# A zero tile for the warm-up products, bn_stats for block 3's second norm, and a new order of operations in an attention and MLP kernel

## The chip, the cores and the metric

The kernel runs on one core of one Trainium2 chip. The metric is device time in microseconds (us), the median over several executions of the whole program; lower is better. A profile is of one execution.

## The reference

The input x has 2048 rows of 448 bf16 numbers. Two residual stages follow each other:

```python
    def _A_ref(x, wqkv, wo):
        B, S, D = x.shape
        H = 16; Dh = D // H
        W, dil = 8, 2
        ...
        off = jnp.arange(W) * dil
        idx = pos[:, None] - off[None, :]
        mask = idx >= 0
        ...
        logits = jnp.einsum("bhsd,bhswd->bhsw", q, kg) * scale
        logits = jnp.where(mask[None, None, :, :], logits, -1e9)
        attn = _softmax(logits, axis=-1)
        o = jnp.einsum("bhsw,bhswd->bhsd", attn, vg)
        return (lambda x, *d: x.transpose(*d))(o, 0, 2, 1, 3).reshape(B, S, D) @ wo

    def _B_ref(x, w1, w2, w3, w4):
        ...
        h = _gelu(_layernorm(x, axis=-1) @ w1)
        ...
        hs = jnp.concatenate([g0, g1, g2, g3], axis=-1) @ w2
        x1 = x + hs
        h2 = _gelu(_layernorm(x1, axis=-1) @ w3) @ w4
        return x1 + h2

    x = A_x
    h = x + _A_ref(_layernorm(x, axis=-1), A_wqkv, A_wo)
    h2 = h + _B_ref(_layernorm(h, axis=-1), B_w1, B_w2, B_w3, B_w4)
```

Each of the 16 heads has 28 columns; a row looks at itself and at the 7 rows that lie 2, 4, ... 14 before it. g0 to g3 are the four column groups of h, moved by 1 and 2 rows forward or back. w3 is 448x1792 and w4 1792x448.

The layer norms have no weights, so one is a mean, a reciprocal root of the variance and one pass over the rows.

## The kernel before

The 2048 rows are cut into four blocks of 512 (four tiles of 128 rows each) for the first part, and into five units of 2, 4, 4, 4 and 2 tiles for the second. One pass over a block consists of these phases, written out in Python as functions:

- `phase_N1`: the first layer norm. Statistics are `bn_stats` and `bn_aggr` on VectorE (`ln_stats`, L513), or, where `STATS` (L15) has an "a", sums that ScalarE or an eviction accumulates (`sums_stats`, L518: a Square pass with an accumulator for each tile). `rstd` (L524) makes the reciprocal root by Ln and Exp on ScalarE (`rs_x`, `rs_y`); `normalize` (L569) writes the normalized tile (`lntm`).
- `phase_A1`, `phase_V`: the normalized rows are turned (for block 0 by 16 products with the identity `ident` on TensorE, `transposed_single`, L617, with two products between them that compute nothing used; for block 1 by products, for blocks 2 and 3 by the DMA's transpose, 'ttdd' in `TURN`), multiplied by wqkv, and evicted from PSUM by ScalarE (`arena<-ps`, `vt<-ps`).
- `phase_A2`: the 8 taps. VectorE multiplies q by the shifted k (`qk_r<-arena`, four products of 2048 or 4096 columns per block), TensorE sums them per head with the 0/1 matrix `zc`, and VectorE makes the softmax (`mx`, `ls`, `pb`).
- `phase_A3`: VectorE spreads the weights into a band (`bd_r<-arena,bmask`), TensorE multiplies by v, `wo_s<-actT` products give the attention's output, and `out()` (L841) evicts it with the residual added, into `xin`. Where `STATS['B1']` has an "a", that eviction is a `scalar_tensor_tensor` which also accumulates the row sum.
- `phase_B1` (L860): the second norm, by `ln_stats` or `sums_stats`; its rows are turned by DMA, and the w1 products and gelu follow (tag M).
- `phase_B2` (L915): the mixer's products with w2 (`w_a`, `w_s`), evicted by a `scalar_tensor_tensor` on VectorE into `arena`, the third norm, and an addition of the residual for each tile, on GpSimd (POOL) or VectorE. `phase_W3` (L962): the w3 products (`ps<-actT,arena`), gelu on ScalarE into `h3T`. `phase_B3` (L979): the w4 products (`ps<-arena,h3T`), a last eviction on VectorE into `ost`, and the store.

Before all of it `setup` (L629) writes masks and identities, and `warm` (L673) issues `WARM` (L61) products of 128x512 through `keep_busy` (L669) that compute nothing used. They read `ident`, which POOL makes by a memset and an `affine_select` (L428 and L429).

**What sets the order.** The phases only declare operations, numbered as they are declared (873 of them). `_Sched.arrange` (L197) then takes the table `ORDER` (L24), one global sequence of all these numbers, and gives each engine its own operations in that sequence; buffers and PSUM banks are handed out in that sequence too. `OTHER` (L56) lists operations that go to their second engine. `_emit_plan` (L250) puts the semaphore waits. Each engine runs its list strictly in that order. `emit_engine` (L1039) also loads ScalarE's table for Exp and Ln (rows of L1043) where the next operation needs another than the last; a load in the other direction is put by the compiler. All other rows of the profile have one line, L1048 (the call that issues an instruction), so they are told apart by their tiles.

## Time and profile before

| quantity | value |
|---|---|
| median of three runs | 189.56 us (188.63 to 190.37) |
| the profiled execution's own time | 188.72 us |
| its span, first to last instruction | 187.0 us |
| TensorE (PE) busy | 180.0 us, 96% |
| VectorE (DVE) busy | 130.8 us, 70% |
| ScalarE (ACT) busy | 124.0 us, 66% |
| GpSimd (POOL) busy | 20.9 us, 11% |
| moved by DMA | 18.29 MB |

The span is 1.7 us shorter than the execution's own time, and the execution lies 0.84 us below the median. In the timeline a row gives the start, the length, the engine, the line, the operation, the tiles (out<-in) with their shape, the number of instructions joined in it, and in brackets how long the engine had been idle before it and what ended that. In the chain of waits a row gives a start, a length, and the engine whose work the end of the program followed from at that time.

### The profile page before, as it was taken

The page shows a single profiled execution, that of the slowest core. Times are in us where ns is not written, and L with a number is a line of the kernel's source. Part 1 is how long each engine was busy: PE and PEld are TensorE (multiplying, and loading weights), DVE is VectorE, ACT ScalarE, POOL GpSimd, SP SyncE. Part 2 cuts the span into 40 slices and gives each one's busy share as a digit, 9 for nine tenths or more (in the row PEclk, how much of TensorE's full clock was granted, in tenths as well). Part 3 has the DMA queues.
Part 4 walks back from the last instruction along what each step waited for, and adds up shares of the span by engine and source line. Part 5 has one row for each costly group of instructions (what it writes and reads, how often), then busy time and mean ns, then how long its engine had stood idle before and what let it go on. Part 6 is the DMA issues. An engine that isn't in the chain of part 4 may idle for free.

```text
span 187.0 us, 5742 instructions
## 1 busy us (share of the span) xinstructions
PE 180.0 (96%) x2482; PEld 93.5 (50%) x2482; DVE 130.8 (70%) x236; ACT 124.0 (66%) x280; POOL 20.9 (11%) x56
## 2 busy tenths in 40 slices
PE   5999999989999989999999999999999999999994
PEld 2685443345453445467455444555444544555663
DVE  7989999999999999999997960089962080000512
ACT  4459989879999999998991987930267004930340
POOL 3440000000003000500042000020034050000000
PEclk9999999999999999999999999999999999999999
DMA  5923583661654697597409060043305031000022
GB/s 151 340 101 58 125 173 63 141 149 17 115 124 94 160 206 301 100 316 146 101 4 140 2 137 4 0 31 84 100 4 112 4 71 60 4 0 0 4 98 74
DMA packets 38609, 18.29 MB, mean 98 GB/s; under 512 B 27464, under 2 KB 38072, under 8 KB 38584
## 3 DMA queue, kind: packets, MB, share of 16 engines
q1 hardware_dynamic: 38584, 17.93, 41.4%
q8 instruction: 19, 0.31, 0.7%
q14 instruction: 6, 0.05, 0.1%
HBM read 8.14 MB, written 1.84 MB: 53 GB/s over the span
## 4 chain that ended last, share of the span: by engine, by line
PE 75%; DVE 16%; ACT 6%; issue 1%; POOL 0%; POOLq 0%
PE ps L1048 75%; DVE bd_r L1048 6%; DVE qk_r L1048 4%; DVE lntm L1048 2%; ACT lntm L1048 1%; DVE xin L1048 1%; DVE st L1048 1%; ACT arena L1048 1%; DVE mx L1048 1%; ACT h3T L1048 1%; ACT L1048 1%; ACT L1043 1%; DVE arena L1048 1%; ACT xin L1048 1%; DVE pb L1048 0%
## 5 line engine op out<-in xcount | busy, mean ns | idle before, releaser
L1048 PE MATMUL ps<-actT,arena 64*128 64x512 bf16 (+2 forms) x812 | 69.6, 326 | 0.3
L1048 ACT ACTIVATE h3T<-ps 128x512 bf16<-128x512 f32 (+1 forms) x70 | 30.7, 520 | 39.1 <-PE ps L1048 38.7
L1048 PEld LDWEIGHTS ps<-actT,arena 64*128 64x128 bf16 (+1 forms) x812 | 35.7, 96 | 29.8 <-PE ps L1048 1.6
L1048 PE MATMUL ps<-arena,h3T 64*128 64x448 bf16 (+3 forms) x434 | 44.5, 343 | 0.0
L1048 DVE SCALAR_TENSOR_TENSOR ost<-ps,mrs,arena 128x448 bf16<-128x448 f32 (+2 forms) x17 | 10.7, 649 | 35.5 <-PE ps L1048 26.9
L1048 ACT ACTIVATE arena<-ps 128x512 bf16<-128x512 f32 (+4 forms) x62 | 31.5, 568 | 2.6 <-PE ps L1048 2.4
L1048 DVE TENSOR_TENSOR qk_r<-arena 128x4096 bf16<-128x4096 bf16 (+1 forms) x16 | 32.1, 2015 | 0.3 <-PE ps L1048 0.3
L1048 PEld LDWEIGHTS ps<-arena,h3T 64*128 64x128 bf16 (+1 forms) x434 | 22.4, 94 | 19.6 <-ACT h3T L1048 0.3
L1048 DVE TENSOR_TENSOR bd_r<-arena,bmask 80x2048 bf16<-80x2048 bf16 x16 | 18.9, 1211 | 0.3 <-ACT arena L1048 0.3
L1048 DVE TENSOR_SCALAR lntm<-arena,mv,rs_y 128x512 bf16<-128x512 f32 x14 | 6.8, 540 | 13.1 <-ACT rs_y L1048 11.6
L1048 POOL TENSOR_TENSOR arena<-arena,xin 128x448 f32<-128x448 f32 x9 | 10.6, 1193 | 34.3 <-DVE lntm L1048 34.3
L1048 PE MATMUL ps<-wo_s,actT 64*128 64x448 bf16 x128 | 14.3, 350 | 0.1
L1048 PE MATMUL ps<-w_s,arena 64*128 64x448 bf16 x88 | 13.3, 350 | 0.0
L1048 PE MATMUL ps<-actT,w_s 64*128 64x512 bf16 (+1 forms) x112 | 13.3, 376 | 0.0
L1048 ACT ACTIVATE lntm<-xin,nm 128x448 bf16<-128x448 bf16 x16 | 10.5, 660 | 4.0 <-DVE nm L1048 4.0
L1048 ACT ACTIVATE actT<-ps 128x512 bf16<-128x512 f32 (+2 forms) x19 | 11.8, 639 | 2.0 <-PE ps L1048 1.9
L1048 PE MATMUL ps<-arena,actT 64*128 64x448 bf16 x112 | 12.6, 350 | 0.1
L1048 DVE SCALAR_TENSOR_TENSOR arena<-xin,rs_y,ps 128x448 f32<-128x448 bf16 x16 | 10.3, 673 | 0.3 <-PE ps L1048 0.3
L1048 DVE BATCH_NORM_STATS2 st<-xin 128x6 f32<-128x448 bf16 x16 | 9.1, 612 | 0.5 <-DMA xin<-in_A_x_dram 0.4
L1048 ACT ACTIVATE vt<-ps 128x448 bf16<-128x448 f32 x16 | 8.4, 543 | 1.0 <-PE ps L1048 1.0
L1048 PEld LDWEIGHTS ps<-wo_s,actT 64*128 64x128 bf16 x128 | 5.9, 94 | 6.1 <-PE ps L1048 0.9
L1048 PEld LDWEIGHTS ps<-actT,w_s 64*128 64x128 bf16 (+1 forms) x112 | 6.0, 98 | 5.6 <-ACT h3T L1048 0.2
(75 smaller groups left out, 167.1 us busy)
## 6 DMA issues: line engine op xcount, KB each, us to landing
arena<-in_B_w_dram SPq DMA_DIRECT2D x2, 896.0 KB, 7.0
out_dram<-ost SPq DMA_DIRECT2D x15, 112.0 KB, 1.8
arena<-in_B_w_dram SPq DMA_DIRECT2D x2, 784.0 KB, 5.8
vw<-vt SPq DMA_DIRECT2D x4, 320.0 KB, 4.1
vw<-vt SPq DMA_DIRECT2D x4, 256.0 KB, 3.5
arena<-in_A_wqkv_dram SPq DMA_DIRECT2D x2, 448.0 KB, 4.5
xin<-in_A_x_dram SPq DMA_DIRECT2D x2, 448.0 KB, 5.1
xin<-in_A_x_dram SPq DMA_DIRECT2D x3, 224.0 KB, 5.3
```

The source lines that it names most:

```text
L1043: eng.preload_act_table_set("natural_log_exp_and_others")
L1048: inst = getattr(eng, meth)(**kw)
```

## The change

First, POOL writes a tile of zeros, `blank`, before anything else, and the products of `keep_busy` (the warm-up and the two between block 0's transposes) read it instead of `ident`; there are 10 warm-up products instead of 9. Second, the second norm of block 3 takes its statistics with `bn_stats` and `bn_aggr` on VectorE: 4 Square passes of ScalarE go, 4 + 4 instructions on VectorE come, and the four evictions ahead of them become `tensor_tensor` without an accumulator. Third, `ORDER` and `OTHER` are new. There are 879 operations.

```diff
-STATS = {'N1': 'vvva', 'B1': 'avaa', 'B2': 'avvvv'}
+STATS = {'N1': 'vvva', 'B1': 'avav', 'B2': 'avvvv'}
...
 ORDER = """
-41 42 0 4 1 7 44 45 46 8 43 6 60 61 9 65 66 2 62 63 64 11 10 72 70 73 71 67 68 69 5 74 75 77 96 98 84 51 52 53 54 55
+0 52 53 54 55 56 57 58 59 60 61 8 42 43 1 2 6 9 62 63 46 3 64 10 67 68 69 12 11 74 72 75 73 65 66 70 71 76 77 78 101
...
 OTHER = """
-103 196 198 510 513 564 565 627 629 699 700 701 769 830
+105 200 201 512 570 571 634 635 704 707
 """
 FULL = (4,)
 FILL = (1, 1, 0, 0)
-WARM = 9
+WARM = 10
...
         ident = sb("ident", [128, 128], BF16)
+        blank = sb("blank", [128, 128], BF16)
...
+        pool("memset", ap=blank[:], constant=0.0)
         pool("memset", ap=ident[:], constant=0.0)
...
         def keep_busy(after=()):

-            return mm(busy(), ident[:], bass.AP(ident, 0, [[128, 128], [0, 4], [1, 128]]), True, True, 512, after)
+            return mm(busy(), blank[:], bass.AP(blank, 0, [[128, 128], [0, 4], [1, 128]]), True, True, 512, after)
```

Three places show what the new table moves. The line number of the issuing call is L1050 in the changed kernel (L1045 for the table of Exp and Ln).

**VectorE, the start** (`st` and `mv` are the statistics of the first norms, `lntm` the normalized tiles, `qk_r` the first products of q and k). Before:

```order
L1048 TENSOR_SCALAR lntm<-xin,mv,rs_y 128x448
L1048 BN_STATS st<-xin 128x6 x2
L1048 BN_AGGR mv<-st 128x2 x2
L1048 TENSOR_SCALAR lntm<-xin,mv,rs_y 128x448
L1048 MEMSET vt 128x128x2
L1048 TENSOR_SCALAR lntm<-xin,mv,rs_y 128x448 x2
L1048 COPY actT<-ps 128x512
L1048 BN_STATS st<-xin 128x6 x4
L1048 BN_AGGR mv<-st 128x2 x4
L1048 TENSOR_SCALAR lntm<-xin,mv,rs_y 128x448 x4
L1048 BN_STATS st<-xin 128x6 x4
L1048 TENSOR_TENSOR qk_r<-arena 128x4096
```

In the changed kernel:

```order
L1050 BN_STATS st<-xin 128x6 x2
L1050 BN_AGGR mv<-st 128x2 x2
L1050 TENSOR_SCALAR lntm<-xin,mv,rs_y 128x448 x4
L1050 TENSOR_REDUCE bmask<-ls 80x4x8
L1050 COPY actT<-ps 128x512
L1050 TENSOR_REDUCE bmask<-ls 80x4x8
L1050 MEMSET pb 128x320
L1050 BN_STATS st<-xin 128x6 x4
L1050 BN_AGGR mv<-st 128x2 x4
L1050 TENSOR_SCALAR lntm<-xin,mv,rs_y 128x448 x4
L1050 TENSOR_TENSOR qk_r<-arena 128x4096
L1050 BN_STATS st<-xin 128x6 x4
```

All four tiles' statistics now stand ahead of the first normalization, the two `bmask` reductions and the memset of `pb` have moved behind the normalizations, and block 2's four `BN_STATS` have moved from ahead of the first `qk_r` product to behind it.

**VectorE, the evictions of unit 1's mixer** (`arena<-xin,rs_y,ps`, which free PSUM banks for the w3 products of unit 0) among block 2's second norm (`lntm<-xin,nm,rs_y`) and block 3's softmax (`mx`, `ls`). Before:

```order
L1048 TENSOR_TENSOR qk_r<-arena 128x2048
L1048 SCALAR_TENSOR_TENSOR arena<-xin,rs_y,ps 128x448
L1048 TENSOR_REDUCE mx<-ps 128x64
L1048 TENSOR_TENSOR ls<-ps,mx 128x512
L1048 TENSOR_TENSOR mrs<-nm,rs_y 128x4
L1048 SCALAR_TENSOR_TENSOR arena<-xin,rs_y,ps 128x448
L1048 TENSOR_SCALAR lntm<-xin,nm,rs_y 128x512 x4
L1048 SCALAR_TENSOR_TENSOR arena<-xin,rs_y,ps 128x448 x2
```

In the changed kernel:

```order
L1050 TENSOR_TENSOR qk_r<-arena 128x2048
L1050 SCALAR_TENSOR_TENSOR arena<-xin,rs_y,ps 128x448
L1050 TENSOR_REDUCE mx<-ps 128x64
L1050 SCALAR_TENSOR_TENSOR arena<-xin,rs_y,ps 128x448
L1050 TENSOR_TENSOR ls<-ps,mx 128x512
L1050 SCALAR_TENSOR_TENSOR arena<-xin,rs_y,ps 128x448 x2
L1050 TENSOR_SCALAR lntm<-xin,nm,rs_y 128x512 x4
```

The third and fourth eviction now stand ahead of the four normalizations. On TensorE the eight w3 products that stood between the two pairs of mixer products now stand behind them, with the rest of unit 0's (62 + 8 before, 70 in one row now); behind the last w3 product that waits for VectorE there are 20 of them before and 40 now.

**ScalarE, block 3's second norm** (`lntm,mv<-xin,nm` are its Square passes, `h3T` unit 1's gelu evictions). Before:

```order
L1048 ACTIVATE actT<-ps 128x512 x2
L1043 ACT_TABLE_LOAD
L1048 ACTIVATE rs_y<-rs_x 128x4
L1048 ACTIVATE lntm,mv<-xin,nm 128x448 x4
L1048 ACTIVATE rs_x<-mv,epsilon 128x4
L1048 ACTIVATE rs_y<-rs_x 128x4
L1048 ACT_TABLE_LOAD
L1048 ACTIVATE h3T<-ps 128x512 x14
```

In the changed kernel:

```order
L1050 ACTIVATE actT<-ps 128x512
L1045 ACT_TABLE_LOAD
L1050 ACTIVATE rs_x<-mv,epsilon 128x4
L1050 ACTIVATE rs_y<-rs_x 128x4
L1050 ACT_TABLE_LOAD
L1050 ACTIVATE h3T<-ps 128x512 x2
L1045 ACT_TABLE_LOAD
L1050 ACTIVATE rs_x<-mv,epsilon 128x4 x2
L1050 ACTIVATE rs_y<-rs_x 128x4
L1050 ACT_TABLE_LOAD
L1050 ACTIVATE h3T<-ps 128x512 x12
```

The Square passes are gone, and the Ln and Exp of block 3's norm stand between the second and the third gelu eviction, with a table load on either side.

58 rows, old and new, of the table ORDER are left out of this document.

## The prediction

> **What bounds the kernel now.** I read the busy table by stages first (a stage's bounds, then for each engine its busy time with the instruction count), then the chain of waits, then TensorE's waits.
>
> ```profile
> 8.40:38.00 29.60, 29.49 (x435) 15.07 (x435) 27.87 (x42) 25.42 (x64) 2.79 (x20) 1.00 0.54 121
> 38.00:86.00 48.00, 45.59 (x880) 23.84 (x877) 47.79 (x73) 45.38 (x106) 4.14 (x6) 1.00 0.62 153
> 86.00:110.00 24.00, 24.00 (x376) 12.43 (x374) 22.33 (x52) 18.96 (x40) 3.29 (x3) 1.00 0.48 81
> 110.00:187.00 77.00, 74.57 (x778) 38.92 (x774) 25.99 (x54) 30.83 (x64) 7.96 (x10) 1.00 0.20 45
> ...
> 2.09 31.15 PE ps L1048 x398
> ...
> 85.39 99.20 PE ps L1048 x1158
> ...
> PE ps L1048 <- POOL ident L1048: 2.1, 1, 2.1
> PE ps L1048 <- DVE bd_r L1048: 1.2, 2, 0.7
> PE ps L1048 <- ACT arena L1048: 0.4, 1, 0.4
> PE ps L1048 <- DVE pb L1048: 0.3, 1, 0.3
> PE ps L1048 <- DVE arena L1048: 0.2, 1, 0.2
> ```
>
> The first number behind the comma is TensorE's busy time, the third VectorE's. From 38 to 86 VectorE has 47.79 of 48.00 us and TensorE 45.59: VectorE paces, and from 8.4 to 38 both are nearly full. In the chain TensorE carries the rest without a break, from 85.39 for 99.20 us. So there are two levers: how soon the work up to 85 us is done, which VectorE decides, and how much TensorE must do from then on. TensorE waits 2.1 us for the identity and 1.2 + 0.4 + 0.3 + 0.2 = 2.1 us for others in the whole program. VectorE's idle time from 8.4 to 86 is 77.60 - 27.87 - 47.79 = 1.94 us, and nothing that only shortens that can bring more.
>
> **Term 1, the start.**
>
> ```profile
> 0.80 0.16 POOL L1048 MEMSET ls<- 80x80 bf16 x1 [0.29 <-POOLq L1075]
> 1.78 0.68 DVE L1048 TENSOR_REDUCE bmask<-ls 80x32 bf16<-80x256 bf16 x2
> 2.09 4.02 PE L1048 MATMUL ps<-ident 128*128 128x512 bf16 x9 [2.09 <-POOL ident L1048]
> 2.47 0.33 DVE L1048 MEMSET pb<- 128x320 uint32 x1
> 4.41 0.40 DVE L1048 TENSOR_SCALAR lntm<-xin,mv,rs_y 128x448 bf16<-128x448 bf16 x1
> 5.78 0.30 DVE L1048 BATCH_NORM_AGGREGATE mv<-st 128x2 f32<-128x6 f32 x2
> 5.91 0.63 PE L1048 MATMUL ps<-ident,lntm 128*128 128x128 bf16 x4
> 6.36 0.27 DVE L1048 MEMSET vt<- 128x256 uint32 x1
> 7.61 0.86 PE L1048 MATMUL ps<-ident,lntm 128*128 128x128 bf16 x8
> 8.40 5.32 PE L1048 MATMUL ps<-actT,arena 64*128 64x256 bf16 x100
> 8.52 2.21 DVE L1048 BATCH_NORM_STATS2 st<-xin 128x6 f32<-128x448 bf16 x4 [0.41 <-DMA xin<-in_A_x_dram]
> ...
> 179.79 4.78 PE L1048 MATMUL ps<-arena,h3T 128*128 128x320 bf16 x36
> ```
>
> POOL's first memset ends at 0.96; with `blank` in that place TensorE begins near 1.05 instead of 2.09. Nine products took 5.91 - 2.09 = 3.82 us, 0.424 each, so ten end near 5.3. This early start is worth nothing by itself, because the first transposes wait for the first normalization. Before, that one began at 4.41 and took 0.31 to the next row; now it stands behind all four statistics, whose last aggregate ended at 6.08 (5.78 + 0.30), less the 0.31 no longer ahead of it: it begins near 5.8 and is through near 6.2. TensorE idles some 0.9 us between.
>
> For VectorE I count up to block 1's statistics. The reductions (0.68) and the `pb` memset (0.33) leave a place where VectorE waited for x, and come behind the normalizations: +1.01. The 0.27 memset goes the other way, and the 0.41 wait for x at 8.52 is filled. The sum is 1.01 - 0.27 - 0.41 = +0.33 us. The bounds are -0.41 (the wait goes, the additions hide) and +1.01 (nothing hides). I take +0.33, since each part has its row. Block 2's `BN_STATS` behind the first `qk_r` only change places with it, and the earlier issue of x's last four tiles hurries data that nobody waits for yet.
>
> The clock. At 7.61 eight products of 128 columns took 8.40 - 7.61 = 0.79 us, 99 ns each; at 179.79, 320 columns took 4.78/36 = 133 ns, or 53 per 128. The half rate therefore ended between 7.6 and 8.4, at most 6.3 us after the first product. The zero products keep TensorE busy as the identity did, and I take the switch to come no later than before.
>
> By the Trainium skill, page "TensorE: Matmul & The Clock Gate", section on the HAM clock gate, the clock is decided in free-running windows of about 3.4 us, and a busy window is needed for the full rate. By that rule the switch falls 3.4 to 6.8 us after the first product of an unbroken stretch, which the 5.5 to 6.3 us of this trace agree with; from 1.05 it would come at 4.5 to 7.9 (an estimate from that page), and the sum would stay as it is.
>
> **Term 2, VectorE's waits up to 85 us.**
>
> ```profile
> 21.25 3.43 DVE L1048 TENSOR_TENSOR qk_r<-arena 128x4096 bf16<-128x4096 bf16 x2 [0.26 <-PE ps L1048]
> 37.03 1.22 DVE L1048 TENSOR_TENSOR bd_r<-arena,bmask 80x2048 bf16<-80x2048 bf16 x1 [0.33 <-ACT arena L1048]
> ```
>
> Two of the waits stand at places that the new order changes. Ahead of the first, block 2's aggregates and block 1's products come in another sequence, with TensorE's value products taken forward; ahead of the second, TensorE's and ScalarE's work for the band stands earlier. I take both as gone: -0.59 us. The bounds are 0 and the whole idle time, -1.94.
>
> **Term 3, unit 1's evictions.**
>
> ```profile
> 78.65 1.70 PE L1048 MATMUL ps<-actT,arena 64*128 64x256 bf16 x28
> 81.31 0.36 PE L1048 MATMUL ps<-w_a,arena 64*128 64x448 bf16 x1 [0.19 <-DVE arena L1048]
> 83.16 1.38 DVE L1048 TENSOR_SCALAR lntm<-xin,nm,rs_y 128x512 bf16<-128x512 bf16 x4
> 84.46 1.27 DVE L1048 SCALAR_TENSOR_TENSOR arena<-xin,rs_y,ps 128x448 f32<-128x448 bf16 x2
> ```
>
> The fourth eviction ended at 85.73 and frees a bank for w3 products. Four normalizations leave the place ahead of it: 84.46 - 83.16 = 1.30 us earlier. But 40 w3 products then stand behind that release where 20 did, at 1.70/28 = 61 ns each: 1.2 us more of TensorE's work. The balance is -0.1 us. TensorE's own count agrees: the same products remain, and at most the 0.19 us wait at 81.31 goes. So -0.1, with bounds 0 and -0.3. The price of the swap is that block 2's normalizations end about 1.2 us later (the two evictions' length), and their turned rows with them; in TensorE's order 14 more w4 products, which term 5 prices, now stand ahead of those that read them, and cover it.
>
> **Term 4, block 3's statistics.**
>
> ```profile
> 87.90 1.67 DVE L1048 BATCH_NORM_STATS2 st<-arena 128x6 f32<-128x448 f32 x3
> 102.83 0.67 ACT L1048 ACTIVATE lntm<-xin,nm 128x448 bf16<-128x448 bf16 x1 [3.84 <-DVE nm L1048]
> 106.13 1.28 ACT L1048 ACT_TABLE_LOAD   x1
> 106.54 1.38 DVE L1048 TENSOR_SCALAR lntm<-xin,nm,rs_y 128x512 bf16<-128x512 bf16 x4
> 113.59 3.19 PE L1048 MATMUL ps<-actT,w_s 64*128 64x512 bf16 x28
> actT<-lntm SPq DMA_TRANSPOSE x11, 4.4
> ```
>
> Four `BN_STATS` at 1.67/3 = 0.56 us and four aggregates at most 0.15 (0.30 for two) are 2.8 us more on VectorE; one eviction of `actT` goes to ScalarE (0.6). ScalarE loses four passes of 0.67 (2.7) and gains two table loads of 1.28 (2.6). All this lies beside TensorE's 24.00 busy us of 24.00 between 86 and 110, which is the cover. The normalizations ended at 107.92, the turn took 4.4, so the rows lay there at 112.3, 1.3 us before the products that read them at 113.59; the 14 w4 products now ahead of those make it 2.6. I take 0 on the path; without the cover it would be about +1.9, by rival C.
>
> **Term 5, the rest.**
>
> ```profile
> 88.55 1.49 PE L1048 MATMUL ps<-arena,h3T 64*128 64x448 bf16 x14
> 89.87 3.19 PE L1048 MATMUL ps<-actT,w_s 64*128 64x512 bf16 x28
> 93.62 2.82 PE L1048 MATMUL ps<-arena,h3T 64*128 64x448 bf16 x28
> 96.38 0.70 PE L1048 MATMUL ps<-bd_r,vw 80*32 80x64 bf16 x64
> ```
>
> Fourteen such products take 89.87 - 88.55 = 1.32 us where the array's shape stays, twice as many 96.38 - 93.62 = 2.76 where another follows (64*128, then 80*32): 0.12 us for a change of shape. I count 54 such changes in TensorE's order before, 49 now; the five that go all lie before 85 us, where VectorE paces, so they bring nothing in this forecast. Residual additions that return to POOL wait for nobody. Behind 113 us both orders hold the same TensorE work: 0.
>
> **The sum.** 0.33 - 0.59 - 0.1 = -0.36 us on the profiled execution's span of 187.0, with 1.7 us around it: 188.72 - 0.36 = 188.36. That execution lies 0.84 below the median, so the median becomes 189.56 - 0.36 = **189.2 us**. One per cent, 1.9 us, is about what a measurement of this kernel can tell from no change; the marks are 187.67 and 191.46.
>
> **Rivals.**
>
> A, VectorE stops pacing. If the new order holds its results ready each time, TensorE gets back its 2.1 us of waits and the five changes of shape, 5 x 0.12 = 0.6: 189.56 - 2.7 = **186.9 us**. For it speaks that from 8.4 to 38 TensorE has 29.49 of 29.60 and so is nearly the bound; against it VectorE's 47.79 of 48.00 from 38 to 86, where the new order removes no work of its own except a few additions.
>
> B, the clock comes late, which makes it slower than before. The place is the gap of 0.9 us between the last warm-up product and the first transpose, which the trace of before does not have (5.91 follows the ninth product directly); or zeros do not count as work. Then the count begins at 6.2 and the full rate comes up to 6.3 us later, at 12.5. The first transposes run at half rate until near 8.8, and the wqkv products until 12.3 or so: 3.5 us at half rate, 1.75 lost, and the first `qk_r` waits for them. 189.2 + 1.75 = **190.95 us**. It decides as soon as the switch falls behind 8.8. For it speaks that the gap is real by the rows of term 1; against it that 4.25 us of products without a break lie ahead of the gap. By the same section of the Trainium skill's page, a window spoilt by the gap could put the switch as late as 6.2 + 6.8 = 13.0, an estimate; no run here shows a gap yet.
>
> C, block 3's statistics hold up the evictions. VectorE has only 24.00 - 22.33 = 1.67 us free from 86 to 110, and 2.8 - 0.6 = 2.2 more to do. If banks come free late, or the turned rows land over 2.6 us later, TensorE stands. The price goes up to the extra work less what is free early in the stage; with the 0.3 us that fits beside 96 us, 1.9: 189.2 + 1.9 = **191.1 us**. Against it: VectorE has 25.99 of 77 us behind 110.
>
> **How the numbers follow.** My forecast has a chance of 0.50, A 0.24, B 0.16, C 0.10; each carries about 1 us on either side. Faster by over 1%: 0.06 from the forecast's edge (terms 1 and 2 at their good bounds), 0.21 from A: 0.27. Slower by over 1%: 0.03 from the forecast, 0.06 from B, 0.04 from C: 0.13. Within 1%: 0.60. The range reaches to A at 187.0 and to C at 191.1, which leaves about half of A and some of B and C outside, 2 in 10.
>
> **What would show it.** Right: TensorE's first product near 1.05, a gap before the first transpose near 6.2, TensorE without a break from about 85 us, and its waits still near 2 us. Term 1 is wrong if block 1's statistics start before 8.5 or behind 9.5, term 2 if the waits on `ps` and `arena` stay, term 4 if TensorE idles between 95 and 115. B shows as products of 256 columns at twice their time behind 8.8 us; A as TensorE waits near zero from 8 to 85 us. A time below 187.7 or above 191.5 makes the forecast wrong.

## The result, and the profile after

The changed kernel takes 190.67 us, median of 20 executions (189.6 to 192.29), against 189.47 us (188.38 to 190.37, 20 executions) for the kernel before it. The ratio is 1.0072 with a 95% interval of 1.0055 to 1.0089: 0.7% or some 1.2 us slower. The forecast was 189.2 us, a little faster. The profiled execution took 190.96 us with a span of 189.2; before, it was 188.72 with 187.0. So the two profiles lie 2.2 us apart, 1 us more than the medians: the profiled execution of the kernel before was 0.75 us faster than its median, that of the changed kernel 0.29 us slower than its own.

The same views come first that bounded the kernel before. The busy table by stages (bounds, length, then busy time with its count for PE, PEld, DVE, ACT and POOL):

```profile
8.40:38.00 29.60, 29.39 (x425) 15.65 (x421) 27.93 (x43) 24.55 (x62) 2.82 (x24) 1.00 0.51 115
38.00:86.00 48.00, 44.44 (x866) 22.34 (x860) 47.48 (x68) 43.81 (x104) 4.97 (x6) 1.00 0.66 162
86.00:110.00 24.00, 23.57 (x382) 12.95 (x378) 21.95 (x48) 17.30 (x34) 1.02 (x1) 1.00 0.41 67
```

VectorE still paces up to 86 us. Its idle time there is 77.60 - 27.93 - 47.48 = 2.19 us, where the forecast wanted the 1.94 of before to shrink to 1.35. (The bound at 8.40 cuts the first wait of before, 0.41 us ahead of 8.52; counted whole it adds 0.29, and the idle time is the same.) TensorE is no longer full from 86 to 110: 23.57 of 24.00. The waits of TensorE and the end of the chain show where:

```profile
PE ps L1050 <- DVE pb L1050: 1.4, 1, 1.4
PE ps L1050 <- POOL blank L1050: 1.1, 1, 1.1
PE ps L1050 <- ACT actT L1050: 1.0, 2, 0.7
PE ps L1050 <- DVE lntm L1050: 0.7, 1, 0.7
PE ps L1050 <- DMA actT<-lntm: 0.3, 1, 0.3
...
87.34 5.93 DMA actT<-lntm
93.31 6.04 PE ps L1050 x114
...
101.80 3.48 DMA arena<-arena
105.33 81.50 PE ps L1050 x842
```

Without the 1.1 us for `blank` TensorE's waits add up to 4.6 us (three rows below 0.7 are not shown), where the forecast wanted them to stay near 2. Before, one piece of TensorE carried the chain from 85.39 to the end. Now two transfers stand in it, a turn of 5.93 us and a copy of 3.48, and TensorE's last unbroken piece begins at 105.33.

The copy is the last of three that unit 2's `w_a` products read. The new table moves them on SyncE's queue too (SPq), which the three places shown with the change leave out. Before, they were issued at 94.80, ahead of a turn at 97.45 and a store at 99.49. In the changed kernel they stand behind both, so they wait until the store's data are there:

```profile
94.80 2.13 SPq L1048 DMA_DIRECT2D arena<-arena  x3
...
100.59 1.80 SPq L1050 DMA_DIRECT2D arena<-arena  x3
104.43 0.83 PE L1050 MATMUL ps<-actT,arena 64*128 64x512 bf16 x6
105.33 0.36 PE L1050 MATMUL ps<-w_a,arena 64*128 64x448 bf16 x1
```

From the six products to the next row it is 0.90 us here, and 0.65 in another execution of the same kernel (x4_after_again below, 103.30 to 103.95), where the copies are in time. So this wait is 0.25 us.

The start, on TensorE and then on VectorE:

```profile
1.06 4.45 PE L1050 MATMUL ps<-blank 128*128 128x512 bf16 x10 [1.06 <-POOL blank L1050]
6.20 0.40 PE L1050 MATMUL ps<-ident,lntm 128*128 128x128 bf16 x4 [0.70 <-DVE lntm L1050]
8.22 3.34 PE L1050 MATMUL ps<-actT,arena 64*128 64x256 bf16 x58 [0.37 <-DVE bmask L1050]
...
2.87 0.63 DVE L1050 BATCH_NORM_STATS2 st<-xin 128x6 f32<-128x448 bf16 x1 [0.73 <-DMA xin<-in_A_x_dram]
5.78 1.39 DVE L1050 TENSOR_SCALAR lntm<-xin,mv,rs_y 128x448 bf16<-128x448 bf16 x4
8.77 2.21 DVE L1050 BATCH_NORM_STATS2 st<-xin 128x6 f32<-128x448 bf16 x4 [0.29 <-DMA xin<-in_A_x_dram]
11.86 1.32 DVE L1050 TENSOR_SCALAR lntm<-xin,mv,rs_y 128x448 bf16<-128x448 bf16 x4 [0.60 <-ACT rs_y L1050]
```

The start is as drawn: the first product at 1.06, the first normalization at 5.78, a gap of 0.70 us, the first transposes at 6.20. Zero products do wake the clock: the first four transposes take 0.40 us, where before they took 0.63, and the 58 wqkv products behind them 58 ns each (3.34/58). What the start costs is small. Block 1's normalizations begin at 11.86 instead of 11.61: VectorE now waits 0.73 us for the first x, where the mask reductions stood, and still 0.29 for block 1's. But the arrival of x moves this row by more than that: in the nine profiles below with VectorE's start of before and the old sequence to 62 us or further it begins between 11.23 and 12.34.

The rest of VectorE's waits up to 85 us (those of 0.15 us and more):

```profile
23.65 0.17 DVE L1050 TENSOR_SCALAR nm<-mv 128x4 f32<-128x4 f32 x1 [0.20 <-ACT lntm L1050]
25.18 2.29 DVE L1050 TENSOR_TENSOR qk_r<-arena 128x4096 bf16<-128x4096 bf16 x1 [0.22 <-PE ps L1050]
32.35 0.69 DVE L1050 TENSOR_REDUCE mx<-ls 128x64 f32<-128x512 f32 x1 [0.19 <-ACT ls L1050]
37.14 1.22 DVE L1050 TENSOR_TENSOR bd_r<-arena,bmask 80x2048 bf16<-80x2048 bf16 x1 [0.17 <-ACT arena L1050]
38.53 0.69 DVE L1050 TENSOR_REDUCE mx<-ps 128x64 f32<-128x512 f32 x1 [0.17 <-PE ps L1050]
50.13 0.17 DVE L1050 TENSOR_SCALAR nm<-mv 128x4 f32<-128x4 f32 x1 [0.18 <-ACT xin L1050]
```

Before there were five waits of this size from 8.4 us on (0.41, 0.60, 0.26, 0.42, 0.33), 2.02 us together. Now there are eight: 0.29 + 0.60 above and 0.20 + 0.22 + 0.19 + 0.17 + 0.17 + 0.18 = 1.13 here, again 2.02. The wait for TensorE ahead of a `qk_r` product stands at 25.18 instead of 21.25, the one ahead of `bd_r` is halved, and those at 32.35, 38.53 and 50.13 are new. In these two profiles the waits were cut into more pieces, not removed.

**What nobody waits for in these rows, and still costs 1.0 of the 2.2 us between the profiles.** VectorE's third and fourth normalization of block 1, and GpSimd's work beside them:

```profile
57.02 1.74 DVE L1050 TENSOR_SCALAR lntm<-xin,nm,rs_y 128x512 bf16<-128x512 bf16 x2
...
56.21 1.10 POOL L1050 COPY w_s<-w_s 128x192 bf16<-128x192 bf16 x1 [44.86 <-DMA w_s<-in_B_w_dram]
57.26 1.35 POOL L1050 MEMSET w_a<- 16x1344 bf16 x1
```

Two normalizations took 1.74 us. They end at 58.76, just behind the memset's end at 58.61. In another execution of the same changed kernel (run x4_after_again below), GpSimd's copy came 1.35 us later, because its weights landed later:

```profile
57.05 0.73 DVE L1049 TENSOR_SCALAR lntm<-xin,nm,rs_y 128x512 bf16<-128x512 bf16 x2
...
57.56 0.41 POOL L1049 COPY w_s<-w_s 128x192 bf16<-128x192 bf16 x1 [46.20 <-DMA w_s<-in_B_w_dram]
57.92 1.21 POOL L1049 MEMSET w_a<- 16x1344 bf16 x1
```

Here the pair takes 0.73 us and the memset begins behind it. Meeting the memset costs VectorE 1.74 - 0.73 = 1.0 us, as a longer instruction, not as a wait. By the Trainium skill, page "SBUF — State Buffer", section "Who interferes with whom", `tensor_scalar` can take both of VectorE's port pairs, of which GpSimd uses one, and whichever engine issues first keeps it until its instruction ends. The trace agrees: the second normalization ends 0.15 us behind the memset. The same section says that an operation with two inputs in SBUF holds up a GpSimd instruction that reads there. The rows agree in that the copy took 1.10 us here beside a `qk_r` product and 0.41 where none ran.

**A ruler for what follows.** From VectorE's third `qk_r` product of block 3 on, the end of the program is nearly fixed. Its row and TensorE's last group, in the kernel before and then in the changed one:

```profile
77.24 3.42 DVE L1048 TENSOR_TENSOR qk_r<-arena 128x4096 bf16<-128x4096 bf16 x2
...
178.97 5.60 PE L1048 MATMUL ps<-arena,h3T 128*128 128x320 bf16 x42
```

```profile
78.97 3.42 DVE L1050 TENSOR_TENSOR qk_r<-arena 128x4096 bf16<-128x4096 bf16 x2
...
181.31 5.50 PE L1050 MATMUL ps<-arena,h3T 128*128 128x320 bf16 x42
```

VectorE is 1.73 us late at that product, and TensorE's last group ends 2.24 us later (186.81 against 184.57). So three quarters of the difference between the two profiles are made ahead of 77 us, and 0.5 us behind it.

### The profile page after: what moved, and what is told of

Same layout as the page of the kernel before. It is cut to its first block, busy times and chain, and to the rows that moved or that the text cites. A ratio compares the mean times of both kernels' runs of the same rounds, so it can differ in the third digit from the quotient of the medians.

```text
span 189.2 us, 5742 instructions
## 1 busy us (share of the span) xinstructions
PE 180.5 (95%) x2483; PEld 93.7 (50%) x2483; DVE 131.1 (69%) x236; ACT 125.0 (66%) x275; POOL 23.5 (12%) x60
## 4 chain that ended last, share of the span: by engine, by line
PE 73%; DVE 11%; DMA 6%; ACT 6%; SPq 1%; issue 1%; DVEq 0%
PE ps L1050 73%; ACT arena L1050 4%; DMA actT<-lntm 3%; DVE lntm L1050 2%; DMA arena<-arena 2%; DVE bd_r L1050 2%; DVE st L1050 2%; DVE qk_r L1050 2%; DMA xin<-in_A_x_dram 1%; SPq L1050 1%; ACT L1050 1%; DVE arena L1050 1%; DVE mx L1050 1%; ACT xin L1050 1%; DVE ost L1050 1%
## 5 line engine op out<-in xcount | busy, mean ns | idle before, releaser
L1050 PE MATMUL ps<-actT,arena 64*128 64x512 bf16 (+2 forms) x812 | 69.0, 325 | 0.4 <-DVE bmask L1050 0.4
L1050 ACT ACTIVATE h3T<-ps 128x512 bf16<-128x512 f32 (+1 forms) x70 | 30.9, 518 | 37.8 <-PE ps L1050 37.4
L1050 PEld LDWEIGHTS ps<-actT,arena 64*128 64x128 bf16 (+1 forms) x812 | 37.0, 96 | 29.2 <-PE ps L1050 1.6
L1050 PE MATMUL ps<-arena,h3T 64*128 64x448 bf16 (+3 forms) x434 | 44.5, 343 | 0.0
L1050 DVE SCALAR_TENSOR_TENSOR ost<-ps,mrs,arena 128x448 bf16<-128x448 f32 (+2 forms) x17 | 10.6, 651 | 38.9 <-PE ps L1050 36.2
L1050 ACT ACTIVATE arena<-ps 128x512 bf16<-128x512 f32 (+4 forms) x62 | 31.9, 567 | 5.1 <-PE ps L1050 4.5
L1050 DVE TENSOR_TENSOR qk_r<-arena 128x4096 bf16<-128x4096 bf16 (+1 forms) x16 | 32.2, 2015 | 0.2 <-PE ps L1050 0.2
L1050 PEld LDWEIGHTS ps<-arena,h3T 64*128 64x128 bf16 (+1 forms) x434 | 22.6, 94 | 19.6 <-issue 0.2
L1050 DVE TENSOR_TENSOR bd_r<-arena,bmask 80x2048 bf16<-80x2048 bf16 x16 | 18.9, 1215 | 1.0 <-ACT arena L1050 1.0
L1050 PE MATMUL ps<-wo_s,actT 64*128 64x448 bf16 x128 | 14.8, 350 | 1.1 <-ACT actT L1050 1.0
L1050 ACT ACTIVATE actT<-ps 128x512 bf16<-128x512 f32 (+2 forms) x20 | 12.0, 644 | 4.2 <-PE ps L1050 4.2
L1050 POOL TENSOR_TENSOR arena<-arena,xin 128x448 f32<-128x448 f32 x12 | 12.1, 1034 | 20.4 <-DVE lntm L1050 17.9
L1050 PE MATMUL ps<-actT,w_s 64*128 64x512 bf16 (+1 forms) x112 | 13.6, 376 | 0.3 <-DMA actT<-lntm 0.3
L1050 PE MATMUL ps<-w_s,arena 64*128 64x448 bf16 x88 | 13.3, 350 | 0.0
L1050 PE MATMUL ps<-arena,actT 64*128 64x448 bf16 x112 | 13.2, 350 | 0.1
L1050 DVE TENSOR_SCALAR lntm<-arena,mv,rs_y 128x512 bf16<-128x512 f32 x14 | 7.1, 548 | 8.7 <-ACT rs_y L1050 6.8
L1050 DVE BATCH_NORM_STATS2 st<-xin 128x6 f32<-128x448 bf16 x20 | 11.5, 615 | 1.1 <-DMA xin<-in_A_x_dram 1.0
L1050 DVE SCALAR_TENSOR_TENSOR arena<-xin,rs_y,ps 128x448 f32<-128x448 bf16 x16 | 10.3, 672 | 2.7 <-PE ps L1050 2.7
L1050 PEld LDWEIGHTS ps<-wo_s,actT 64*128 64x128 bf16 x128 | 5.8, 94 | 7.6 <-ACT actT L1050 1.6
L1050 ACT ACTIVATE rs_x<-mv,epsilon 128x4 f32<-128x4 f32 (+2 forms) x16 | 4.6, 296 | 6.5 <-DVE mv L1050 6.4
```

Of the source, the lines that this page charges most:

```text
L1050: inst = getattr(eng, meth)(**kw)
```

## The experiments

All versions compute the whole reference. Each ratio is to the kernel before, run beside it on the same chip, with its 95% interval. The table gives the ruler of one profiled execution each: start of the third `qk_r` product, end of TensorE's last group, and the distance between them.

| version | ratio | third qk_r | end | distance |
|---|---|---|---|---|
| the kernel before | 1 | 77.24 | 184.57 | 107.33 |
| the changed kernel | 1.0072 [1.0055, 1.0089] | 78.97 | 186.81 | 107.84 |
| x4_after_again | 1.0065 [1.0028, 1.0101] | 78.04 | 185.42 | 107.38 |
| y4_both | 1.0028 [1.0004, 1.0052] | 77.90 | 185.49 | 107.59 |
| c62_old_to_62 | 1.0026 [0.9997, 1.0056] | 77.52 | 185.09 | 107.57 |
| c80_old_to_80 | 1.0035 [1.0008, 1.0062] | 78.00 | 185.64 | 107.64 |
| c85_old_to_85 | 1.0009 [0.9984, 1.0034] | 77.12 | 184.81 | 107.69 |
| c92_old_to_92 | 1.0000 [0.9976, 1.0024] | 77.76 | 185.57 | 107.81 |

**One part of the change at a time.** First the zero tile and the tenth warm-up product alone, in the kernel before:

```diff
-WARM = 9
+WARM = 10
...
+        pool("memset", ap=blank[:], constant=0.0)
...
-            return mm(busy(), ident[:], bass.AP(ident, 0, [[128, 128], [0, 4], [1, 128]]), True, True, 512, after)
+            return mm(busy(), blank[:], bass.AP(blank, 0, [[128, 128], [0, 4], [1, 128]]), True, True, 512, after)
```

> The kernel before with the zero tile and ten warm-up products alone. TensorE starts near 1.05 and reaches the full rate before its first transposes are through, so the wqkv products can start near 7.9 instead of 8.40. If TensorE's start counts: 0.3 to 0.5 us faster, ratio 0.997 to 0.999. If VectorE paces there: 1.000. If the earlier start costs something: above 1.002.

Measured: 1.0004 [0.9983, 1.0025]. This part is worth nothing and costs nothing that can be measured.

Then both this and block 3's `bn_stats`, in the old sequence on all engines, with the statistics ahead of the four evictions that follow them:

```diff
-STATS = {'N1': 'vvva', 'B1': 'avaa', 'B2': 'avvvv'}
+STATS = {'N1': 'vvva', 'B1': 'avav', 'B2': 'avvvv'}
```

> The zero tile, the tenth warm-up product and bn_stats for block 3's second norm, but the order of the kernel before: the new instructions stand at the places of those that they replace. If the new order is the loss (theories 1 and 2): ratio to the kernel before 0.996 to 1.002. If bn_stats on VectorE is the loss (theory 3, rival C of the prediction): 1.005 to 1.010, with TensorE waiting between 95 and 115 us.

Measured: 1.0099 [1.0069, 1.0128], no better than the whole change. TensorE and VectorE in that place:

```profile
106.45 9.02 PE L1049 MATMUL ps<-actT,arena 64*128 64x512 bf16 x82 [1.59 <-DVE arena L1049]
...
102.54 2.19 DVE L1049 BATCH_NORM_STATS2 st<-xin 128x6 f32<-128x448 bf16 x4
105.13 2.45 DVE L1049 SCALAR_TENSOR_TENSOR arena<-xin,rs_y,ps 128x448 f32<-128x448 bf16 x4
```

The evictions begin at 105.13 (before: 102.72), and TensorE stands 1.59 us for them. That is rival C of the prediction, near its price of 1.9 us (0.0099 of 189.29; the medians are 1.45 apart), in the old sequence. With the statistics behind the evictions instead:

```diff
+L1049 SCALAR_TENSOR_TENSOR arena<-xin,rs_y,ps 128x448 x4
 L1049 BN_STATS st<-xin 128x6 x4
 L1049 BN_AGGR mv<-st 128x2 x4
 L1049 TENSOR_SCALAR nm<-mv 128x4
-L1049 SCALAR_TENSOR_TENSOR arena<-xin,rs_y,ps 128x448 x4
```

> Zero tile, ten warm-up products and bn_stats with the order of the kernel before, as in the run with the old order (ratio 1.0099, TensorE waited 1.59 us for VectorE's evictions at 106 us), but block 3's statistics behind the four evictions of unit 2's mixer. Theory 5 (bn_stats costs only where it stands ahead of evictions): the wait of 1.59 us goes, ratio 0.999 to 1.003, unless the turned rows of block 3 come late: then TensorE waits for the turning DMA near 113 us and the ratio is 1.004 or more.

Measured: 1.0069 [1.0041, 1.0097]. The wait moves to ScalarE:

```profile
110.83 4.94 PE L1049 MATMUL ps<-actT,arena 64*128 64x512 bf16 x42 [1.25 <-ACT h3T L1049]
...
107.84 0.30 ACT L1049 ACTIVATE rs_x<-mv,epsilon 128x4 f32<-128x4 f32 x1 [8.40 <-DVE mv L1049]
```

ScalarE stands 8.40 us in front of the reciprocal root, with the gelu evictions queued behind it, and TensorE waits 1.25 us for one of those. So `bn_stats` needs the new sequence in this part of the program; with it, TensorE has no such wait. What the new sequence does here is pay for the statistics that were added.

**The same kernel again, and GpSimd's memset.** Theory: the meeting with the memset makes part of the loss, in those executions in which it happens. Rival: the start's sequence does. The changed kernel once more, unedited:

> The changed kernel once more, unaltered, for a second profile beside the others of this call. In its first profile VectorE's second normalization of block 1 took 1.38 us instead of 0.40 while a GpSimd memset of 1.35 us ran beside it. Theory 1 (the two engines exclude each other there, and that is most of the loss): the same long row again near 57 us, ratio to the kernel before 1.005 to 1.009. Theory 2 (the loss is the sum of many small waits on VectorE and of two waits of TensorE for DMA behind 86 us, 0.29 and 0.25 us): the same ratio with a normalization of 0.4 us.

Measured: 1.0065 [1.0028, 1.0101]; three of seven executions took 189.56 to 189.58 us, four 190.37 to 191.79. The profiled one took 189.56, without the meeting. Its ruler is 78.04: the meeting's 0.93 us are gone and 0.80 are left. Next the memset alone is issued ahead of the last copy into `zc`, then behind the first write to `epsilon`, then there with the start restored:

```diff
 L1049 MEMSET arena 1x2
+L1049 MEMSET w_a 16x1344
 L1049 COPY zc<-ls 128x32
 L1049 COPY w_s<-w_s 128x4x3x16
-L1049 MEMSET w_a 16x1344
```

> The changed kernel with one operation moved: GpSimd writes the zeros of w2's last rows behind its setup work near 15 us instead of behind the copy of w1 near 57 us. Theory 1: the normalization takes 0.4 us again and the kernel gains 1.0 us, ratio to the kernel before 1.000 to 1.003. Theory 2: no change against the changed kernel, ratio 1.005 to 1.009.

```diff
 L1049 MEMSET epsilon 128x1
+L1049 MEMSET w_a 16x1344
 L1049 MEMSET arena 64x16
...
 L1049 COPY w_s<-w_s 128x4x3x16
-L1049 MEMSET w_a 16x1344
```

> The changed kernel with GpSimd's memset of w2's last rows at 2.3 to 3.5 us, where VectorE runs no normalization (in the run before this one it stood near 11 us and met one there too: 0.76 us instead of 0.38). Theory 1: the normalization at 57 us takes 0.4 us in every execution; the median falls by the part of the executions that met it, 0.3 to 0.6 us, and the spread of the times shrinks; ratio 1.002 to 1.005. If the meeting is a rarity: 1.005 to 1.009.

Measured: 1.0049 [1.0026, 1.0073] and 1.0045 [1.0019, 1.0070]. In both profiles the normalizations at 57 to 58 us take 0.75 us, as they should. In the profiled execution of the first, the early place made a new meeting (the normalizations at 11.82 took 1.67 us instead of 1.31), and the clock came late:

```profile
6.29 0.61 PE L1049 MATMUL ps<-ident,lntm 128*128 128x128 bf16 x4 [0.79 <-DVE lntm L1049]
8.96 3.89 PE L1049 MATMUL ps<-actT,arena 64*128 64x256 bf16 x58
```

Four transposes took 0.61 us instead of 0.40, and 58 products 67 ns each over the whole group instead of 58. That is rival B in one execution. Three of its twelve executions took 190.85 us and more (190.85, 190.99 and 191.28, the profiled one), the others 189.38 to 190.24. In the second, two of twelve executions (190.94 and 191.38) stood apart from the other ten (189.22 to 190.03). To try whether the gap does it, three more warm-up products close it:

```diff
-WARM = 10
+WARM = 13
```

> The changed kernel with the memset first (ratio 1.0045, two of twelve executions at 190.9 and 191.4) and 13 warm-up products instead of 10, which fill the gap of 0.9 us ahead of the first transpose. If the gap makes the clock switch late in some executions (in one profile the wqkv products from 8.96 to 12.69 took 67 us for 1000 of 256 columns instead of 58): no execution above 190.4, the median falls by 0.1 to 0.3 us. If those executions have another cause: no change.

(Where this expectation speaks of 67 and 58, ns for each product are meant.) Measured: 1.0050 [1.0031, 1.0068], seven executions of 189.56 to 190.43, none apart.

```profile
1.06 5.14 PE L1049 MATMUL ps<-blank 128*128 128x512 bf16 x13 [1.06 <-POOL blank L1049]
6.26 0.40 PE L1049 MATMUL ps<-ident,lntm 128*128 128x128 bf16 x4
```

The gap is closed, and the median stays (189.91 against 189.89). Seven executions without an outlier, where two of twelve had been apart, prove nothing. So the late clock is seen in one profile, how often it comes is open, and it is no large part of the median.

**The start put back.** VectorE's start in the sequence of before, with ScalarE's to match:

```diff
 L1049 MEMSET wo_s 128x896
+L1049 TENSOR_REDUCE bmask<-ls 80x4x8 x2
+L1049 MEMSET pb 128x320
 L1049 BN_STATS st<-xin 128x6
 L1049 BN_AGGR mv<-st 128x2
 L1049 BN_STATS st<-xin 128x6
 L1049 BN_AGGR mv<-st 128x2
+L1049 TENSOR_SCALAR lntm<-xin,mv,rs_y 128x448
 L1049 BN_STATS st<-xin 128x6 x2
 L1049 BN_AGGR mv<-st 128x2 x2
...
```

> The changed kernel with VectorE's start as before: both bmask reductions and the memset of pb ahead of the first statistics, the first normalization ahead of the statistics of tiles 2 and 3, the memset of vt behind the second normalization; all else is the new order. Theory 4 (VectorE now idles 0.7 us until x lands and does that work later): 0.6 us less than the changed kernel, and no gap on TensorE before 4.9 us, so no execution whose clock switches late; ratio to the kernel before 1.001 to 1.004. If the loss lies behind 20 us: as the changed kernel, 1.005 to 1.009.

Measured: 1.0051 [1.0027, 1.0075], in two groups: six executions of 189.6 to 189.86 us and six of 190.5 to 191.45. The profiled one is of the second group, and in it the normalizations met the memset (1.73 us, third `qk_r` at 78.94). Both together:

> Both of the last two edits. If the start (0.6) and the meeting (0.3 to 0.6) make the loss: as the kernel before or a little faster, ratio 0.997 to 1.002. If the new order costs something else behind 20 us: 1.003 or more.

Measured: 1.0028 [1.0004, 1.0052], all twelve executions between 189.35 and 190.19 us. The second group is gone. So the meeting is shown as the cause of about 1 us in those executions in which it happens: both profiles with it have the ruler at 78.94 and 78.97, and in none of the profiles with the memset elsewhere are the normalizations at 57 us long. With the start restored the slow group goes with it. With the changed kernel's start some executions still stand apart (three and two of twelve, above), so there it is not the only cause. In the ratios the memset's place is worth some 0.4 us (1.0051 to 1.0028 with the start restored; 1.0072 and 1.0065 to 1.0045 without); single steps of this size lie within the intervals.

Moving the memset in the kernel before gives nothing. There the pair is through before it, by 0.19 to 0.74 us in the four profiles that have the old sequence and the memset at its old place:

```diff
 L1047 MEMSET epsilon 128x1
+L1047 MEMSET w_a 16x1344
...
 L1047 COPY w_s<-w_s 128x4x3x16
-L1047 MEMSET w_a 16x1344
```

> The kernel before with GpSimd's memset of w2's last rows near 3 us instead of behind the copy of w1 near 58 us. If that memset meets VectorE's normalizations in some executions of the kernel before too: the slowest executions (190 and more) go, ratio 0.997 to 0.999. If it meets them in the new order alone: no change, 0.9985 to 1.0015.

Measured: 1.0022 [0.9997, 1.0046]; no gain.

**Two places of the sequence put back alone.** In y4_both, block 2's normalizations ahead of unit 1's third and fourth eviction again, so that the turned rows are early:

```diff
+L1049 TENSOR_SCALAR lntm<-xin,nm,rs_y 128x512 x4
 L1049 SCALAR_TENSOR_TENSOR arena<-xin,rs_y,ps 128x448 x2
-L1049 TENSOR_SCALAR lntm<-xin,nm,rs_y 128x512 x4
```

> The kernel with VectorE's start restored and the memset first (ratio 1.0028), and block 2's four normalizations ahead of the third and fourth eviction of unit 1's mixer again, as before the change: term 3 of the prediction undone on VectorE, with TensorE's new order kept. If the later turned rows are the price (TensorE waited 0.30 us for them at 92.27): that wait goes, and nothing else, 0.3 us faster. If the earlier evictions were worth something in the new order of TensorE: TensorE waits up to 1.1 us for VectorE's evictions between 84 and 87 us, 0.5 to 1 us slower.

Measured: 1.0081 [1.0062, 1.0100]. The wait for turned rows goes, and a larger one comes:

```profile
86.45 2.60 PE L1049 MATMUL ps<-actT,arena 64*128 64x256 bf16 x40 [1.14 <-DVE arena L1049]
```

The 40 w3 products that the new sequence of TensorE puts behind the fourth eviction now wait 1.14 us for it. The swap on VectorE answers a need that the same table makes on TensorE; beside the 1.14 us, the 0.3 us for turned rows is the cheaper end. And, also in y4_both, VectorE's order between 30 and 35 us as before, to take the small waits away:

```diff
 L1049 TENSOR_TENSOR ls<-ps,mx 128x512
-L1049 TENSOR_SCALAR lntm<-xin,nm,rs_y 128x512 x4
+L1049 TENSOR_TENSOR qk_r<-arena 128x4096
+L1049 TENSOR_SCALAR lntm<-xin,nm,rs_y 128x512
 L1049 TENSOR_REDUCE mx<-ls 128x64
-L1049 TENSOR_TENSOR qk_r<-arena 128x4096
+L1049 TENSOR_SCALAR lntm<-xin,nm,rs_y 128x512 x3
```

> The same base (ratio 1.0028), with VectorE's order between 30 and 35 us as before the change: the qk_r product ahead of the four normalizations of block 3, so that ScalarE's exponentials are ready when the sum mx reads them. Theory 6 (what is left is many waits of some 0.2 us on VectorE, in new places): the wait of 0.19 us at 32.3 goes and VectorE is 0.2 to 0.3 us earlier from there on; whether TensorE ends earlier by as much shows whether VectorE still paces.

Measured: 1.0191 [1.0167, 1.0214].

```profile
33.21 2.29 DVE L1049 TENSOR_TENSOR qk_r<-arena 128x4096 bf16<-128x4096 bf16 x1 [1.75 <-PE ps L1049]
...
38.13 0.49 PE L1049 MATMUL ps<-ident,pb 64*80 64x64 bf16 x16 [1.71 <-DVE pb L1049]
```

`qk_r` needs a buffer back from TensorE's products with `zc`, which come later in the new sequence. The one small wait that was tried could not be taken out alone: an engine's order is good or bad only beside the others'.

**The cut.** So all engines were cut at once: `ORDER` follows the old sequence up to VectorE's work of 21, 37, 62, 80, 85 or 92 us, and the new one for all that is left, with the zero tile, `bn_stats` and the early memset kept. The first row of the table, as it is in the cuts from 62 us on:

```diff
 ORDER = """
-0 52 53 54 55 56 57 58 59 60 61 8 42 43 1 2 6 9 62 63 46 3 64 10 67 68 69 12 11 74 72 75 73 65 66 70 71 76 77 78 101
+0 42 43 1 5 2 8 45 46 47 9 44 7 62 63 10 67 68 3 37 64 65 66 12 11 74 72 75 73 69 70 71 6 76 77 79 98 100 86 52 53 54
...
```

> Blank, zeros' memset early and bn_stats as in the version with both repairs; every engine follows the old sequence up to VectorE's work of 21 us and the new sequence behind it. Theory (the loss left over accrues in VectorE's small waits between 30 and 78 us, about 0.6 us, and 0.3 us at block 2's turned rows): ratio 1.003 to 1.005, VectorE's third qk_r product of block 3 at about 78 us, 0.6 to 0.8 later than in the kernel before. Rival 1 (what is lost is lost in the start's sequence): ratio 1.000. Rival 2 (what is lost is lost behind 80 us): ratio 1.003 too, but VectorE at 77.2 to 77.4 as before.

> The same with the old sequence up to VectorE's work of 37 us. Theory: the 0.3 us that the new sequence had lost by 40 us is not lost, ratio 1.001 to 1.004, VectorE's third qk_r product of block 3 0.3 to 0.5 us later than before. Rival 2 (loss behind 80 us): ratio 1.003, VectorE as before.

> The same with the old sequence up to VectorE's work of 62 us. Theory: most of VectorE's 0.6 us is not lost, ratio 1.000 to 1.003, third qk_r product of block 3 0.1 to 0.3 us later than before, wait for block 2's turned rows 0.3 us remains. Rival 2: ratio 1.003 with VectorE as before.

> The same with the old sequence up to VectorE's work of 80 us, the new one behind it with bn_stats for block 3. Theory: ratio 0.999 to 1.002, VectorE at 80 us as before, a wait of 0 to 0.3 us for block 2's turned rows, no break of TensorE between 95 and 115. Rival 2 (the loss lies behind 80 us, in the sequence of TensorE's last part): ratio 1.003 or more, with TensorE's busy time behind 110 us longer or waits there.

The first two miss: 1.0141 [1.0114, 1.0169] and 1.0201 [1.0169, 1.0232]. The seam itself costs more than what was sought. With the cut at 37:

```profile
40.10 1.22 DVE L1049 TENSOR_TENSOR bd_r<-arena,bmask 80x2048 bf16<-80x2048 bf16 x1 [3.65 <-ACT arena L1049]
```

VectorE waits 3.65 us for an eviction that ScalarE has in another place in the one sequence than in the other; with the cut at 21 it waits 1.55 us for a Square pass at 26.49. These two runs tell nothing about the loss. With the cuts at 62 and 80 the seam is clean, and the ratios are 1.0026 [0.9997, 1.0056] and 1.0035 [1.0008, 1.0062], no better than the 1.0028 of y4_both: by the ratios, then, the old sequence up to there brings nothing back. The profile of the first says otherwise:

```profile
8.83 2.21 DVE L1049 BATCH_NORM_STATS2 st<-xin 128x6 f32<-128x448 bf16 x4 [0.71 <-DMA xin<-in_A_x_dram]
...
91.87 1.90 PE L1049 MATMUL ps<-actT,w_s 64*128 64x512 bf16 x16 [0.29 <-DMA actT<-lntm]
```

VectorE is 0.28 us late at the ruler, and has been since x landed 0.31 us later (8.83 against 8.52); from block 1's normalizations to the ruler it takes 65.60 us, against 65.63 before, 66.10 in x4_after_again and 66.32 in y4_both. So in this execution the old sequence does win back the half microsecond that VectorE loses there, and 0.24 us of distance, with the wait for turned rows, remain. The other profiles agree. With the old sequence up to 62 us or further this way takes 65.34 to 65.90 us in six (the kernel before, x1, z2 and the cuts at 62, 85 and 92; versions are named by the first part of their names). With the new one, where the normalizations meet no memset, it takes 66.00 to 66.32 us in five (x4, y3, y4, y5 and w1). The two groups don't touch. In the other three of the old sequence (x2, z1 and the cut at 80, 66.09 to 66.62) TensorE stands 0.57 to 0.85 us near 43 us with nothing in the profile that it waits for. The eleven executions of the cut at 62 in its ratio spread from 188.98 to 191.05 us, too far for a ratio to show it. For the cut at 80 that stand, 0.85 us at 42.6, makes the ruler useless. Two further cuts ask for the rest:

> The old sequence on every engine up to VectorE's work of 85 us, so unit 1's third and fourth eviction stand behind block 2's normalizations again; the new sequence and bn_stats for block 3 behind it. Theory (the 0.25 us that remain with the cut at 62 and 80 are the wait for block 2's turned rows): no wait for turned rows at 92 us, end of the program 107.3 to 107.4 us behind the start of the third qk_r product of block 3, ratio 0.998 to 1.002. Rival (what remains lies behind 86 us, in bn_stats and the last part's sequence): ratio 1.003, end 107.6 us behind that product.

> The same with the old sequence up to VectorE's work of 92 us. Theory: as with 85, ratio 0.998 to 1.002, and no wait for turned rows. Rival: ratio 1.003 or more, with a wait of TensorE for arena or h3T between 95 and 115 us where the old sequence and block 3's additional statistics meet.

Measured: 1.0009 [0.9984, 1.0034] and 1.0000 [0.9976, 1.0024]. The ratios fall as the theory said, and there is no wait for turned rows in either profile. But the distances, 107.69 and 107.81, don't fall to 107.3 to 107.4: that half of the expectation missed. The kernel before and then the cut at 85:

```profile
83.27 3.82 PE L1048 MATMUL ps<-actT,arena 64*128 64x256 bf16 x62
...
83.15 4.33 PE L1049 MATMUL ps<-actT,arena 64*128 64x256 bf16 x62
86.98 97.84 PE ps L1049 x1136
```

TensorE's unbroken piece begins at 86.98, not at 85.39 as before: its 62 w3 products at the seam take 0.51 us longer. In the profile of the cut at 92 it is the three copies again: from the six products to the `w_a` products it is 1.02 us instead of 0.65, which is 0.37 of the 0.48 that its distance is over the kernel before. So what remains behind 77 us lies mostly in one place in each profile, the seam in the one and the queue of transfers in the other; neither is `bn_stats`. What is settled is this: with the old sequence up to 85 us and the memset early, block 3's `bn_stats`, the zero tile and the new last part together cost nothing that can be measured (1.0009 and 1.0000, against 1.0072 [1.0055, 1.0089] with the new sequence throughout, and 1.0045 to 1.0050 with it throughout and the memset early, in x3, y3 and w1). The loss is made ahead of 85 us by the new sequence. How the part that isn't the memset's divides between the start, VectorE's small losses and the turned rows is read from profiles alone; the ratios of the steps between lie within each other's intervals. No version here is faster than the kernel before.

## Why the prediction was wrong, step by step

**What bounds it: right.** VectorE paces up to 85 us, and TensorE from there on.

**Term 1, +0.33: not contradicted, and too small to be shown.** Block 1's normalizations begin 0.25 us later (0.33 in x4_after_again, where they begin at 11.94). But with the start of before the same row moves by 1.1 us with the arrival of x, and putting the start back is worth no more than the intervals hide (1.0045 to 1.0028), so the agreement in size may be luck. One part of it was wrong: the wait of 0.41 us for x is not "filled". 0.29 of it stays, because x does not land at one time; block 1's statistics started between 8.5 and 8.9 us in the profiles of the changed kernel and of y4_both, and at 9.28 in w1_warm13. That the gap of 0.9 us before the transposes would stand there (it was 0.70) and that zeros count as work was right, and the median doesn't show rival B; one profile does.

**Term 2, -0.59: this step failed.** Two waits stood at places that the order changed, and I took them as gone, with a bound of 0 that had no place for a loss. Waits of both kinds are still there (the prediction's own sign that this term is wrong), 0.22 and 0.17 us instead of 0.26 and 0.33, and the eight waits of the new sequence add up to the same 2.02 us as the five of before. I had read who was waited for, but not what becomes late next. For the wait at 37.03 that was ScalarE, which is busy 25 of 30 us in that stage and so is late for something else. And VectorE loses time that no wait shows. From block 1's normalizations to the ruler it issues 93 instructions in both kernels, which took 65.63 us before and 66.10 in x4_after_again, where nothing is met. Their durations add up to 71.25 and 71.37 us, the breaks between them to 1.18 and 1.25; what neighbours overlap falls from 6.80 to 6.52. In the trace an instruction begins before its predecessor has ended; one that is released late begins later without a break showing. What neighbours overlap is 6.68 us or more in all nine profiles with the old sequence up to 62 us or further, and 6.64 or less in all eight of the changed kernel and of x3, x4, y2 to y5 and w1. That the lost overlap is late releases is my reading, not tried by itself; the sums are the traces'. In place of -0.59 stands +0.47 in this pair, and 0.1 to 1.0 between the two groups of profiles (65.34 to 65.90, and 66.00 to 66.32).

**A term that was missing: GpSimd's memset.** Of POOL's work the prediction had the memsets at the start and the residual additions ("wait for nobody"), but not the memset of `w_a`. An instruction of POOL's can also make one of VectorE's longer. The two stood near each other already before: the memset at 58.02, the normalizations through at 57.28. The new sequence put the pair about half a microsecond later. It also lets GpSimd's copy ahead of the memset begin earlier: at 55.54 to 57.56 us in eight profiles with the new sequence (the changed kernel, x3, x4, y2 to y5 and w1), where it is 57.26 to 58.62 in the nine with the old sequence up to there. So the pair now lies in the range over which the arrival of the weights moves the memset. Price: 1.0 us in the executions where they meet. No row of before showed this price; what could be seen was the memset of 1.21 us 0.74 us behind the normalizations.

**Term 3, -0.1: the gain came and was worth nothing.** The third and fourth eviction ended 86.01 - 78.97 = 7.04 us behind the ruler instead of 85.73 - 77.24 = 8.49: 1.45 us earlier, where 1.30 was forecast. But "cover it" failed. The normalizations end at 87.30, 1.03 us later against the ruler, and the turn took 5.93 us, where it had taken 4.8 in the kernel before, with its rows there 0.5 us ahead of need: the rows came 0.29 us too late (0.10 in x4_after_again). Term 3 counted the later start of the turn and not its length. The length goes with the swap: y4_both, and then y5_norms_first, which has the four normalizations first again:

```profile
actT<-lntm SPq DMA_TRANSPOSE x1, 6.0
...
actT<-lntm SPq DMA_TRANSPOSE x1, 4.5
```

In all eight profiles read with the normalizations first this turn takes 4.4 to 4.8 us, in all twelve with the evictions first 5.7 to 6.1. Why the turn is longer there is not shown.

**Term 4, 0: right for the statistics, and only in the new sequence.** TensorE has no wait for VectorE or ScalarE between 95 and 115 us. By the prediction's own sign it should not stand there at all; the 0.25 us ahead of 105.33 come from the three copies on SyncE's queue, which no term had. In the old sequence TensorE waits 1.59 us behind the same statistics, or 1.25 for a gelu eviction: the cover that the term named is what the new order of that part provides.

**Term 5, 0: right as far as the ratios tell.** The cuts at 85 and 92 us leave the last part in the new sequence and give 1.0009 and 1.0000.

**The sum.** In the profiled pair the 1.73 us ahead of the ruler are 0.93 that x4_after_again does not have, the meeting above all, and 0.80 from the start (0.33) and VectorE's way to the ruler (0.47), where 0.33 - 0.59 = -0.26 had been put. The 0.51 behind it are the wait for turned rows (0.29) and that for the copies (0.25). The medians lie 1.2 us apart and not 2.2, because the profiled execution of the kernel before is a fast one of its kernel; how many of the 20 executions of the changed kernel met the memset is not known. Neither rival B nor rival C decided it, though the measured 190.67 lies near their prices. The loss came through several places of 0.25 to 0.5 us and one of 1.0, of which the prediction had only the start.

## What to carry to other kernels

When a new order changes the place of a wait on an engine that is full, count what it adds elsewhere before counting the wait as gone: here the number of waits went from five to eight, their sum stayed at 2.02 us, and another 0.5 us was lost without showing as a wait. For each `tensor_scalar` or copy on VectorE look at what GpSimd does within a microsecond of it, and put GpSimd's long memsets where VectorE has other work, or early, as in y4_both, whose executions lie within 0.9 us of each other. And an order found as a whole is tested as a whole: undoing one place of it on VectorE alone cost 1.0 and 3.1 us against y4_both where TensorE leaned on it (y5_norms_first and s1_s0_order), while the start, put back on VectorE and ScalarE together, cost nothing that can be measured. Look at the queue of the transfers as well: a copy that is issued behind a store waits for the store's data (0.25 us in the profile of the changed kernel).
